# A convolution and an attention on one core: the last chunk's heads in other tiles, another loop behind the loop, and new constants for the planner of the order

## The chip, the cores and the metric

The kernel runs on one core of a Trainium2 chip. A core has TensorE (PE; its weight loads are shown as PEld), VectorE (DVE), ScalarE (ACT), GpSimd (POOL) and SyncE (SP, which here only issues DMAs), each with its own instruction stream, held together by semaphores. The metric is the device time of one execution in microseconds. Before the change it was 1152.21 us, the median of three runs (1152.09 to 1154.93).

## The reference

Two parts that share no data, and whose outputs are laid side by side:

```python
# A: S4 convolution, L = 2048, D = 576 channels, N = 128 states
P = exp(dt * (A_re + i A_im) * l);  K = einsum("dn,dnl,dn->dl", C, P, dt * B).real
y = irfft(rfft(u, 2L) * rfft(K, 2L))[:L] + u * Dskip
# B: attention, S = 2048, 32 query heads of 18, one key head and one value head
q = (x @ wq) in 32 heads;  k = x @ wk;  v = x @ wv
p = softmax(q k^T * 18 ** -0.5);  o = p v
b = concat(o over the heads) @ wo
out = concat([y, b], axis=-1)
```

## The kernel before

**Attention.** The 2048 query rows are cut into four chunks of 512 (`NCH`, `CT`). Within a chunk the 32 heads go in 8 groups of four, and within a group the keys in 16 blocks of 128. One step is one key block of one group: four heads, as two score tiles of 128 x 1024 (`scores`, L533: two matmuls each), two exponentials on ScalarE (`exponentials`, L544), and one product with the values (`product`, L846: four matmuls in four column groups, which add up over the 16 key blocks into one PSUM bank). There are 4 x 8 x 16 = 512 steps and 1024 exponentials. The values have a column of ones, so that each head's softmax denominator is row 18 of its 32 rows. After 16 steps `gather` (L547) copies the group's bank to SBUF and stores it in DRAM (`od`).

**Heads to output.** When a chunk's last group is gathered, `normalize` (L555) loads its denominators (`dn`), takes their reciprocals, stores them (`rden`), loads the heads in five blocks of rows (28 heads in four blocks m = 0 to 3 of 126 rows, the last four heads in block 4), loads each block's reciprocals broadcast over the rows (`db`) and multiplies. `outproj` (L591) then projects with `wo`: 4 row tiles x 2 column halves x 5 blocks, 40 units of one `matmul4` each. The heads lie in a single tile `oT` that all chunks share.

The last chunk is normalised block by block: block m = 0, 1, 2, 3 after groups 1, 3, 5, 6 (`LATE`, L62). Blocks 0 to 2 may be projected in the loop (`outproj_part`, L617) into an SBUF sum `part`; which (tile, half, block) units are still missing stands in `rest`. `finish` (L642) comes behind the loop: it takes the last group from PSUM (`rc_last`, `o_last`), normalises its four heads on chip with a matmul (`bc`), does all units left in `rest` and the last block with its own weights `w4`, adds them to `part` and stores the rows.

**Convolution.** It goes in 12 chunks of 48 channels. `front` (L1287) makes a chunk's kernel from powers and tables, nearly all on VectorE, with a matmul stage `kgen`; `back` (L1360) transforms input and kernel on TensorE, multiplies the spectra on VectorE, transforms back (`iy`) and stores (`outa`). The front of the next chunk and the back of this one run as two streams.

**Order.** TensorE's, ScalarE's and VectorE's orders are written out by a planner in Python when the program is built. It keeps an estimate of each engine's time (`Clock`: `K.t` for TensorE, `K.v` for VectorE, `K.a` for ScalarE) and runs the work beside the scores, exponentials and products as generators (`Stream`): `side` (query projections and output projections), `prepare` (L731: normalising), `tail` (bounds of the scores) and the convolution's streams. A generator yields what it needs next: `"v"` (VectorE, not before an estimated time), `"p"` (TensorE and the one PSUM bank for this work), `"w"` (nothing yet). `fill` (L808) puts such work between scores and products as far as a credit goes. The credit grows with each step by an allowance worked out from `TOTAL`, `LAST` and what was filled so far, between `C1` and `C2` (up to step 384) or `C3`. `RATE` is the pace of VectorE's convolution work per step, `C11` how far it may run ahead; `PACE` is the pace under which the convolution `lags` (L1491), and while it does and has a matmul waiting, no projection is begun unless it is urgent. `late` (L759) says when projections are behind, with `LEFT`. `prepare` starts a chunk's first block only when no output projection is open, and for the last chunk only when also all queries are made (`due`). Behind the loop, normalising is done to its end, then an output projection is finished, then the convolution is drained stream by stream.

Of the kernel before, what the change touches and what calls it, by code (L numbers as in the profile page):

```python
# [9 lines left out]
F32 = mybir.dt.float32  # L10
# [3 lines left out]
ALU = mybir.AluOpType  # L14
# [3 lines left out]
P = 128  # L18
# [25 lines left out]
NP = 10  # L44


RATE = 1.829
PACE = 1.71
AHEAD = 0.752
TOTAL = 429.151  # L50
LAST = 560.514

GAP = 0.437
C1, C2, C3, C4, C5, C6, C7, C8, C9, C10, C11, C12 = 0.529, 1.112, 0.728, 0.947, 0.591, 0.827, 0.566, 0.187, 0.25, 0.502, 47.793, 16.067
DEFER = 0.48
NAUG = 5
SLACK = 3.096
HEAD = 8.716

LEFT = 0.638  # L60

LATE = {1: [0], 3: [1], 5: [2], 6: [3]}  # L62

# [133 lines left out]
class Attention:  # L197
# [357 lines left out]
    def normalize(self, c, ms):  # L555

        nc, V, K = self.nc, self.V, self.k
        od = self.od[c].rearrange("(h r) n -> h r n", r=32)
        if ms[0] == 0:
            self.oT = self.cp.tile([P, 5, CT], F32, tag="oT", name=f"oT{c}")  # L560
        o = self.oT
        h0, h1 = MT[ms[0]][0] // DH, sum(MT[ms[-1]]) // DH
        n = (h1 - h0) * CT // P
        dn = self.p1.tile([P, P], F32, tag="dn", name=f"dn{c}_{h0}")
        rd = self.dr.tile([H, CT], F32, tag="rden", name=f"rden{c}_{h0}")
        nc.sync.dma_start(dn[:n, :], od[h0:h1, DH, :].rearrange("h (a n) -> h a n", n=P))
        yield "v", K.t + 8.0, False
        V.tensor_scalar(dn[:n, :], dn[:n, :], 1e-37, None, op0=ALU.max)
        V.reciprocal(dn[:n, :], dn[:n, :])
        nc.sync.dma_start(rd[h0:h1, :].rearrange("h (a n) -> (h a) n", n=P), dn[:n, :])  # L570
        for m in ms:
            m0, mn = MT[m]
            nc.sync.dma_start(o[:mn, m, :], od[m0 // DH:(m0 + mn) // DH, 0:DH, :])
        yield "v", max(K.v, K.t) + 5.0, False
        tiles = {}

        def fetch(m):
            m0, mn = MT[m]
            tiles[m] = self.p1.tile([P, CT], F32, tag="db", name=f"db{c}_{m}", bufs=2)
            nc.sync.dma_start(tiles[m][:mn, :], rd[m0 // DH:(m0 + mn) // DH, :].unsqueeze(1).broadcast_to([mn // DH, DH, CT]))  # L580
        for m in ms[:2]:
            fetch(m)
        for m in ms:
            mn = MT[m][1]
            yield "v", K.t + 7.0, False
            V.tensor_tensor(o[:mn, m, :], o[:mn, m, :], tiles[m][:mn, :], op=ALU.mult)
            self.scaled[m] = K.v + 0.3
            if m + 2 in ms:
                fetch(m + 2)

    def outproj(self, c):  # L591
        nc, V, K = self.nc, self.V, self.k
        o = self.oT
        self.o_left += 40
        yield "p", max(self.scaled[4], K.fill), False
        for t in range(4):
            ob = self.p1.tile([P, D], F32, tag="ob", name=f"ob{c}_{t}")
            for n in range(2):
                cs = slice(n * 288, (n + 1) * 288)
                ps = self.bank(288, f"op{c}_{t}_{n}")  # L600
                for m, (m0, mn) in enumerate(MT):
                    matmul4(nc, ps, o[:mn, m, t * P:(t + 1) * P], self.wo[:mn, m, cs], start=(m == 0), stop=(m == 4))
                    K.pe(0.485)
                    self.o_left -= 1
# [12 lines left out]
    def outproj_part(self, c, ms, part):  # L617

        nc, V, K = self.nc, self.V, self.k
        o = self.oT  # L620
        self.o_left += 8 * len(ms)
        for t in range(4):
            for n in range(2):
                yield "p", max(self.scaled[ms[-1]], K.fill), False
                cs = slice(n * 288, (n + 1) * 288)
                ps = self.bank(288, f"op{c}_{t}_{n}_{ms[0]}")
                for m in ms:
                    matmul4(nc, ps, o[:126, m, t * P:(t + 1) * P], self.wo[:126, m, cs], start=(m == ms[0]), stop=(m == ms[-1]))
# [12 lines left out]

    def finish(self, c, part, o_ps, w4, b4):  # L642


        nc, V, o = self.nc, self.nc.vector, self.oT
# [7 lines left out]
        def begin(t, nh, tile):  # L653

            ps[t, nh] = tile[:, :288]
            for m in range(4):
                if (t, nh, m) in self.rest:
                    matmul4(nc, ps[t, nh], o[:126, m, t * P:(t + 1) * P], self.wo[:126, m, cols[nh]], start=(m == min(x[2] for x in self.rest if x[:2] == (t, nh))), stop=False)
# [72 lines left out]
    def prepare(self):  # L731

        nc = self.nc
        while True:
# [48 lines left out]
    def main(self, conv, flag):  # L783
# [134 lines left out]
        nc.vector.tensor_scalar(flag, self.ubound[0:1, :], LIMIT / (2 * SCALE) * QQ, None, op0=ALU.is_le)  # L918
        self.finish(NCH - 1, self.part, o_ps, self.w4, self.b4)

# [678 lines left out]
```

## Time and profile before

| | |
|---|---|
| median of the runs | 1152.21 us |
| the profiled execution | 1153.4 us |
| its span (first to last instruction) | 1151.6 us |
| TensorE busy | 1085.5 us (94%) |
| ScalarE busy | 997.1 us (87%) |
| VectorE busy | 988.2 us (86%) |
| last product ends at | 1121.5 us |
| granted TensorE clock, mean | 0.99 |

Times in the views are microseconds from the span's start. A row of the timeline gives start, busy time, engine, line, operation, what is written <- what is read, shapes, how many instructions, and in brackets how long the engine was idle before it and what ended that. Each fp32 matmul stands as two records, so that a unit of an output projection, four matmuls, is eight records. `op` and `fin` are output projections in the loop and in the finish, `ops` the products, `s` the scores, `P` the exponentials. `L120`, `L124`, `L128` and `L140` are the helpers that record VectorE's operations for the planner, `L194` is `matmul4`.

### The profile page before, as it was taken

The numbers are of one execution on the slowest core, as the hardware profiler recorded it, in microseconds if no ns is written. First come the engines' busy times: TensorE is split into PE (matmuls) and PEld (weight loads), VectorE is DVE, ScalarE is ACT, GpSimd is POOL, SyncE is SP. The second block draws the span as 40 slices with busy tenths as digits, with TensorE's granted clock in tenths as the row PEclk, the third lists the DMA queues.
The fourth block names the chain that finished last, engine by engine and source line by source line (L and its number), as shares of the span: only waits on it lengthen the run. The fifth ranks groups of instructions, "written<-read, shape, count | busy, mean of one in ns | idle before, by whom it ended". The sixth has DMA issues, their size and how long they took to land.

```text
span 1151.6 us, 33003 instructions
## 1 busy us (share of the span) xinstructions
PE 1085.5 (94%) x13886; PEld 398.2 (35%) x13886; DVE 988.2 (86%) x1676; ACT 997.1 (87%) x1052; POOL 140.1 (12%) x257
## 2 busy tenths in 40 slices
PE   6989899999999999899999999999988999999996
PEld 2333234334333334333333333334222333333333
DVE  4878998997998998998899898998878898997753
ACT  3878998888989989998878899999999998999980
POOL 5321412133033010000224000000000000000000
PEclk9999999999999999999999999999989999999998
DMA  7412433122224113122212201102221202102111
GB/s 225 140 54 75 136 96 94 33 90 81 62 65 151 33 42 91 42 69 89 80 40 80 92 29 57 61 29 87 64 78 55 72 29 78 47 29 94 30 44 53
DMA packets 59279, 83.37 MB, mean 72 GB/s; under 512 B 14867, under 2 KB 35335, under 8 KB 58613
## 3 DMA queue, kind: packets, MB, share of 16 engines
q1 hardware_dynamic: 47557, 73.24, 19.8%
q0 software_dynamic: 10848, 7.37, 2.5%
q8 instruction: 111, 1.82, 0.7%
q10 hardware_dynamic: 720, 0.58, 0.2%
q14 instruction: 43, 0.35, 0.1%
HBM read 46.59 MB, written 33.85 MB: 70 GB/s over the span
## 4 chain that ended last, share of the span: by engine, by line
PE 63%; ACT 16%; DVE 11%; issue 6%; DMA 2%; POOL 1%; ACTq 0%; DVEq 0%
PE ops L846 25%; PE s L533 17%; ACT P L544 14%; PE op L194 5%; PE q L410 3%; PE kg L1280 3%; PE iy L194 3%; DVE tab L120 2%; PE fin L194 1%; POOL qd L461 1%; PE hk L194 1%; DVE ks L120 1%; DVE acc L120 1%; PE lu L194 1%; PE lk L194 1%
## 5 line engine op out<-in xcount | busy, mean ns | idle before, releaser
L544 ACT ACTIVATE P<-s 128x1024 f32<-128x1024 f32 x992 | 933.0, 1035 | 99.3 <-PE s L533 96.9
L846 PE MATMUL ops<-P,v_sb 128*32 128x512 f32 x4096 | 511.8, 599 | 2.5 <-DVE o L124 2.4
L533 PE MATMUL s<-aug,kaug 55*128 55x512 f16 x2048 | 310.2, 382 | 38.3 <-ACT P L544 32.8
L533 PEld LDWEIGHTS <-kaug 55*128 55x128 f16 x2048 | 93.6, 94 | 360.7 <-issue 317.1
L846 PEld LDWEIGHTS ops<-P,v_sb 128*32 128x32 f32 x4096 | 116.2, 110 | 162.4 <-issue 135.0
L461 POOL DMA_DIRECT2D qd<-qh x116 | 66.1, 577 | 273.8 <-DVE qh L128 271.3
L410 PE MATMUL q<-x,wq_sb 128*32 128x256 f32 x1360 | 83.7, 382 | 1.1 <-DVE ksb L124 0.6
L194 PE MATMUL op<-wo_sb,oT 126*32 126x288 f32 (+1 forms) x1024 | 73.2, 411 | 2.4 <-DVE ob L124 1.8
L1191 POOL MEMSET fr<- 128x192 f32 x24 | 9.8, 491 | 520.3 <-DVE tt L120 303.3
L120 DVE TENSOR_TENSOR tab<-tab,tt 128x576 f32<-128x576 f32 (+1 forms) x72 | 59.1, 821 | 1.7
L120 DVE TENSOR_TENSOR tab<-fr,dif 128x576 f32<-128x576 f32 (+1 forms) x72 | 58.8, 817 | 0.0
L120 DVE TENSOR_TENSOR tab<-sum,fr 128x576 f32<-128x576 f32 (+1 forms) x72 | 58.7, 816 | 0.0
L120 DVE TENSOR_TENSOR tab<-tab 128x576 f32<-128x576 f32 (+1 forms) x72 | 58.7, 815 | 0.0
L120 DVE TENSOR_TENSOR tt<-fr,sum 128x576 f32<-128x576 f32 (+1 forms) x72 | 58.6, 814 | 0.0
L410 PEld LDWEIGHTS q<-x,wq_sb 128*32 128x32 f32 x1360 | 39.5, 109 | 38.7 <-issue 14.2
L124 DVE COPY ksb<-kg 128x192 f32<-128x192 f32 x48 | 17.5, 364 | 40.4 <-PE kg L1280 39.0
L120 DVE TENSOR_TENSOR acc<-acc,pt 128x1728 f32<-128x1728 f32 (+2 forms) x36 | 48.6, 1351 | 0.3
L120 DVE TENSOR_TENSOR pt<-us,ks 128x1728 f32<-128x1728 f32 (+2 forms) x36 | 48.3, 1350 | 0.0
L1280 PEld LDWEIGHTS kg<-tab 128*32 128x32 f32 x2304 | 37.2, 111 | 25.6 <-DVE ksb L124 8.9
L542 ACT ACTIVATE P<-s,bias 128x1024 f32<-128x1024 f32 x32 | 32.9, 1121 | 13.3 <-PE s L533 13.3
L1280 PE MATMUL kg<-tab 128*32 128x64 f32 x2304 | 42.4, 222 | 0.6 <-DVE tab L120 0.3
L120 DVE TENSOR_TENSOR ks<-ks 128x576 f32<-128x576 f32 (+1 forms) x48 | 41.0, 855 | 0.9
(159 smaller groups left out, 1010.9 us busy)
## 6 DMA issues: line engine op xcount, KB each, us to landing
od<-o SPq DMA_DIRECT2D x31, 256.0 KB
aug<-qd SPq DMA_DIRECT2D x124, 55.0 KB
u<-u SPq DMA_DIRECT2D x12, 384.0 KB
kd<-ksb SPq DMA_DIRECT2D x12, 384.0 KB
kt<-kd SPq DMA_DIRECT2D x48, 96.0 KB
outa<-u SPq DMA_DIRECT2D x12, 384.0 KB
pw<-pw SPq DMA_DIRECT2D x8, 528.0 KB
oT<-od SPq DMA_DIRECT2D x16, 252.0 KB
```

The source lines that it names most:

```text
L120: return self.v.tensor_tensor(out, *a, **k)
L124: return self.v.tensor_copy(out, *a, **k)
L194: nc.tensor.matmul(ps[j:e], w[:, j:e], x, start=start, stop=stop, tile_position=(0, j))
L410: nc.tensor.matmul(ps[o, 256 * f:256 * f + 256], w[:, k, i], xt[:, k, x], start=(k == 0), stop=(k == 4), tile_position=(0, 32 * j))
L461: q.dma_start(qd[h:h + n, row + d:row + d + nd, cs], src[i1:i1 + n * nd, :cs.stop - cs.start])
L533: nc.tensor.matmul(ps[:, j, :], self.kaug[r, kb * P:(kb + 1) * P], t[r, :], start=True, stop=True)
L542: nc.scalar.activation(pt, ps, AF.Exp, bias=self.bias, scale=SCALE / QQ)
L544: nc.scalar.activation(pt, ps, AF.Exp, scale=SCALE / QQ)
L846: nc.tensor.matmul(o_ps[32 * j:32 * j + 32, :], self.v[:, kb, :], pts[2 * n + j // 2][:, j % 2, :], start=(kb == 0), stop=(kb == 15), tile ...
L1191: nc.gpsimd.memset(t[:, :, 0:NF:8], one)
L1280: nc.tensor.matmul(ps[32 * g:32 * g + 32, d, :], t[:, :32], t[:, 32:], start=(j == 0), stop=(j == 1), tile_position=(0, 32 * g))
```

## The change

- The last chunk's normalised heads go into the first 512 columns of the tiles that held the query weights of blocks 0 to 3 (`self.heads`), one tile per block; `oT` stays for chunks 0 to 2. For the last chunk `prepare` no longer waits until no output projection is open, only until all queries are made.
- `normalize` gives its steps other estimated times.
- The load of `w4` moves from block 3's preparation to the end of chunk 2's output projection.
- Behind the loop, one loop takes the step of whichever stream has its inputs first: convolution, preparing, and output while block 0 is not fully projected.
- The planner's constants are replaced.

```diff
-RATE = 1.829
-PACE = 1.71
-AHEAD = 0.752
-TOTAL = 429.151
-LAST = 560.514
-
-GAP = 0.437
-C1, C2, C3, C4, C5, C6, C7, C8, C9, C10, C11, C12 = 0.529, 1.112, 0.728, 0.947, 0.591, 0.827, 0.566, 0.187, 0.25, 0.502, 47.793, 16.067
-DEFER = 0.48
+RATE = 1.838
+PACE = 1.856
+AHEAD = 0.729
+TOTAL = 340.0
+LAST = 576.841
+
+GAP = 0.359
+C1, C2, C3, C4, C5, C6, C7, C8, C9, C10, C11, C12 = 0.549, 0.718, 0.83, 1.288, 0.739, 1.059, 0.572, 0.186, 0.382, 0.431, 24.516, 11.926
+DEFER = 0.395
 NAUG = 5
-SLACK = 3.096
-HEAD = 8.716
-
-LEFT = 0.638
+SLACK = 3.285
+HEAD = 13.454
+
+LEFT = 1.086
...
 # normalize
-        if ms[0] == 0:
-            self.oT = self.cp.tile([P, 5, CT], F32, tag="oT", name=f"oT{c}")
-        o = self.oT
+        if c < NCH - 1:
+            oT = self.oT = self.cp.tile([P, 5, CT], F32, tag="oT", name=f"oT{c}")
+            o = [oT[:, m, :] for m in range(5)]
+        else:
+            o = self.heads
...
-        yield "v", K.t + 8.0, False
+        yield "v", max(K.t + 1.0, self.o_free + 4.5) + 4.0, False
...
-            nc.sync.dma_start(o[:mn, m, :], od[m0 // DH:(m0 + mn) // DH, 0:DH, :])
-        yield "v", max(K.v, K.t) + 5.0, False
-        tiles = {}
+            nc.sync.dma_start(o[m][:mn, :], od[m0 // DH:(m0 + mn) // DH, 0:DH, :])
+        yield "v", max(K.v, K.t) + 1.6, False
+        tiles, fetched = {}, {}
 
         def fetch(m):
+            fetched[m] = max(K.t, K.v)
...
-            yield "v", K.t + 7.0, False
-            V.tensor_tensor(o[:mn, m, :], o[:mn, m, :], tiles[m][:mn, :], op=ALU.mult)
+            yield "v", max(K.t, fetched[m] + 4.6), False
+            V.tensor_tensor(o[m][:mn, :], o[m][:mn, :], tiles[m][:mn, :], op=ALU.mult)
...
 # outproj, its end
+        if c == NCH - 2:
+            self.w4 = self.p1.tile([P, D], F32, tag="ob", name="w4")
+            nc.sync.dma_start(self.w4, self.a["wo4"])
...
 # prepare
-            while ms[0] == 0 and (self.outs or c == NCH - 1 and self.due < 1 << 30):
+            while ms[0] == 0 and (self.outs if c < NCH - 1 else self.due < 1 << 30):
                 yield "w", 0.0, False
...
+                self.heads = [w.rearrange("p k n -> p (k n)")[:, :CT] for w in self.wq[:4]]
...
             if ms[0] == 3:
-                self.w4 = self.p1.tile([P, D], F32, tag="ob", name="w4")
                 self.b4 = self.p2.tile([P, P], F32, tag="aw", name="b4")
-                nc.sync.dma_start(self.w4, self.a["wo4"])
                 nc.sync.dma_start(self.b4, self.a["b4"])
...
 # main, behind the loop
-        while self.todo or self.busy or holder() or any(m == 0 for _, _, m in self.rest):
+        while True:
+            conv.turn()
+            h, live = holder(), [st for st in conv.streams if st.live]
             if self.todo or self.busy:
-                prep.advance()
-            elif holder() or self.outs:
-                (holder() or side).advance()
-        conv.drain()
+                live.append(prep)
+            if side.holds or self.outs and any(m == 0 for _, _, m in self.rest):
+                live.append(side)
+            if not live:
+                break
+            able = [st for st in live if st.kind == "v" or st.kind == "p" and h in (None, st)]
+            for st in [min(able, key=lambda st: st.event())] if able else live:
+                if st.live:
+                    K.t = max(K.t, st.event())
+                    st.advance()
```

In `outproj_part` and `finish` the heads' operand `o[:126, m, ...]` becomes `o[m][:126, ...]`.

More of the change, by code (lines that the diff above doesn't have):

```diff
@@ L615, in outproj @@
                 yield "p", K.fill, False
+        if c == NCH - 2:
+            self.w4 = self.p1.tile([P, D], F32, tag="ob", name="w4")
+            nc.sync.dma_start(self.w4, self.a["wo4"])
     def outproj_part(self, c, ms, part):
         nc, V, K = self.nc, self.V, self.k
-        o = self.oT
+        o = self.heads
         self.o_left += 8 * len(ms)
@@ L627, in outproj_part @@
                 for m in ms:
-                    matmul4(nc, ps, o[:126, m, t * P:(t + 1) * P], self.wo[:126, m, cs], start=(m == ms[0]), stop=(m == ms[-1]))
+                    matmul4(nc, ps, o[m][:126, t * P:(t + 1) * P], self.wo[:126, m, cs], start=(m == ms[0]), stop=(m == ms[-1]))
                     K.pe(0.485)
@@ L642, in finish @@
     def finish(self, c, part, o_ps, w4, b4):
-        nc, V, o = self.nc, self.nc.vector, self.oT
+        nc, V, o = self.nc, self.nc.vector, self.heads
         o_sb = self.p2.tile([P, CT], F32, tag="o", name="o_last", bufs=1)
@@ L657, in begin @@
                 if (t, nh, m) in self.rest:
-                    matmul4(nc, ps[t, nh], o[:126, m, t * P:(t + 1) * P], self.wo[:126, m, cols[nh]], start=(m == min(x[2] for x in self.rest if x[:2] == (t, nh))), stop=False)
+                    matmul4(nc, ps[t, nh], o[m][:126, t * P:(t + 1) * P], self.wo[:126, m, cols[nh]], start=(m == min(x[2] for x in self.rest if x[:2] == (t, nh))), stop=False)
         def end(t, nh):
@@ L910, in main @@
             behind += 1
-        while self.todo or self.busy or holder() or any(m == 0 for _, _, m in self.rest):
+        while True:
+            conv.turn()
+            h, live = holder(), [st for st in conv.streams if st.live]
             if self.todo or self.busy:
-                prep.advance()
-            elif holder() or self.outs:
-                (holder() or side).advance()
-        conv.drain()
+                live.append(prep)
[8 more added lines that the diff above has]
+                    st.advance()
+        self.left = len(self.rest)
+        self.left = len(self.rest)
         nc.vector.tensor_scalar(flag, self.ubound[0:1, :], LIMIT / (2 * SCALE) * QQ, None, op0=ALU.is_le)
```

## The prediction

> **What bounds the kernel now.** I read the page's busy times first, then the busy time by stretch, then who waited for whom, and last the timeline of the end and of the places where the stretches are thin. In the rows of stretches stand the stretch, its length, the busy time (and instructions) of PE, PEld, DVE, ACT and POOL, the granted clock and the DMA.
>
> ```profile
> span 1151.6 us, 33003 instructions
> PE 1085.5 (94%) x13886; PEld 398.2 (35%) x13886; DVE 988.2 (86%) x1676; ACT 997.1 (87%) x1052; POOL 140.1 (12%) x257
> ...
> 832.00:864.00 32.00, 27.06 (x237) 7.75 (x229) 24.37 (x52) 29.82 (x31) 0.80 (x2) 0.89 0.23 78
> 864.00:896.00 32.00, 27.99 (x300) 7.91 (x298) 29.05 (x43) 31.36 (x35) 0.80 (x2) 1.00 0.19 61
> 896.00:928.00 32.00, 30.20 (x424) 11.66 (x420) 26.51 (x58) 29.09 (x32) 0.00 (x0) 1.00 0.19 60
> ...
> 1056.00:1088.00 32.00, 30.73 (x386) 11.30 (x386) 20.43 (x34) 29.72 (x33) 0.00 (x0) 1.00 0.19 61
> 1088.00:1120.00 32.00, 30.44 (x318) 9.91 (x310) 21.12 (x32) 30.25 (x33) 0.00 (x0) 1.00 0.11 39
> ...
> 0.00:1121.50 1121.50, 1065.86 (x13630) 388.95 (x13634) 979.35 (x1660) 996.36 (x1050) 140.14 (x257) 0.99 0.24 73
> 1121.50:1151.60 30.10, 19.61 (x264) 9.24 (x252) 8.80 (x16) 0.77 (x2) 0.00 (x0) 0.84 0.15 51
> ```
>
> TensorE is the bound: 1085.5 of 1151.6 us, and the change leaves its matmuls the same in kind and number. So only its idle 66 us can be won, or grow: 55.6 before 1121.5, and 10.5 of the 30.1 us behind the loop, where ScalarE has almost nothing to do. In 864 to 896 the roles are swapped: ScalarE has 31.36 of 32 us and TensorE is 4.0 us short, because there is no filler (query projection, output projection, convolution) to put between the exponentials.
>
> ```profile
> PE s L533 <- ACT P L544: 32.8, 98, 2.4
> ...
> PE fin L194 <- DVE flag L918: 4.9, 1, 4.9
> ```
>
> The first row is that shortage summed over the loop, 98 small waits. The second is one wait behind it:
>
> ```profile
> 1093.12 0.68 DVE L124 COPY o<-ops 128x512 f32<-128x512 f32 x1
> ...
> 1119.62 1.90 PE L846 MATMUL ops<-P,v_sb 128*32 128x512 f32 x16
> ...
> 1120.24 0.20 DVE L128 TENSOR_SCALAR dn<-dn 28x128 f32<-28x128 f32 x1
> ...
> 1120.48 0.94 DVE L140 RECIPROCAL dn<-dn 28x128 f32<-28x128 f32 x1
> ...
> 1122.79 0.77 SPq L580 DMA_DIRECT2D db<-rden  x1
> 1126.62 0.69 DVE L120 TENSOR_TENSOR oT<-oT,db 126x512 f32<-126x512 f32 x1 [5.19 <-DMA db<-rden]
> ...
> 1127.29 0.40 DVE L675 TENSOR_SCALAR rc_last<-ops 128x256 f32<-128x256 f32 x1
> ...
> 1127.36 4.07 PE L194 MATMUL fin<-wo_sb,oT 126*32 126x288 f32 x32 [4.87 <-DVE flag L918]
> ```
>
> The last product ends at 1121.52, but the fourth block of heads (m=3) is only then normalised, through two transfers, and VectorE holds `rc_last`, the first step of the finish, behind it until 1127.29.
>
> **The change, part by part.** *Own tiles for the last heads.* Before, `prepare` (L740) lets the last chunk's first block start only when no output projection is left; the four blocks then follow one another.
>
> ```profile
> L566 SPq DMA_DIRECT2D dn<-od x4: 729/755/779, 930.3 to 1103.7; - x4
> L128 DVE TENSOR_SCALAR dn<-dn x4: 203/204/208, 1055.6 to 1120.2; 28x128 f32<-28x128 f32 x4
> ...
> L194 PE MATMUL op<-wo_sb,oT x320: 403/406/431, 927.3 to 1043.7; 126*32 126x288 f32 x128, 72*32 72x288 f32 x32
> ...
> L410 PE MATMUL q<-x,wq_sb x1360: 378/379/404, 34.7 to 614.6; 128*32 128x256 f32 x195
> ```
>
> The first denominators were asked for at 930.3 and divided at 1055.6, 125 us later, when chunk 2's projection (927.3 to 1043.7) was out of the way. Afterwards the only condition is that all queries are made; their last matmul is at 614.6, so I cost the new tiles' own waits at nothing (if the queries slip past step 416, the first block waits for them). The instructions of a block are the same: two on the denominators, one product, four transfers on SP. They are issued earlier, among the aug loads, which are made a group or more ahead. The load of `w4` moves as well, to the end of chunk 2's projection, into the tile that the last output row leaves: SP stands at it until that row is stored, with aug loads behind it. They have a group's time, over 30 us; without that the scores would wait about the 3.8 us of the `db` load below. Cost: nothing. So blocks 0 to 2 can be ready soon after groups 1, 3 and 5. For block 3, whose group's copy ends at 1093.8, the new allowances give 0.3+4.5+4.0 to the denominators, 1.2 for dividing, 1.6 and 4.6 to the product: 16.2 us, so 1110, and the loop ends at 1121.5. **Gain: the finish starts at the last product, 1127.3-1121.5 = 5.8 us.**
>
> *The clock behind the wait.*
>
> ```profile
> 816.59 2.15 PE L194 MATMUL op<-wo_sb,oT 126*32 126x288 f32 x32
> ...
> 851.35 0.39 PE L533 MATMUL s<-aug,kaug 55*128 55x512 f16 x2 [2.42 <-ACT P L544]
> ...
> 853.72 3.64 PE L846 MATMUL ops<-P,v_sb 128*32 128x512 f32 x16
> ```
>
> The 32 matmuls behind the wait took 4.07 us against 2.15 for the same 32 in the loop. **Gain: 1.9 us.** But a finish with fewer units is sparser, and a slow stretch in it is as likely: bounds 0 and +4.7 (its 64 `w4` matmuls at the 1.18 us per 16 quoted below, doubled). I take **+1.9**, the price of one such stretch, which is the nearest row. [...]
>
> *Units that leave the finish.*
>
> ```profile
> L194 PE MATMUL fin<-wo_sb,oT x192: 403/406/691, 1121.3 to 1143.6; 126*32 126x288 f32 x192
> ...
> L194 PE MATMUL op<-wo_sb,oT 126*32 126x288 f32 x320 | 23.3, 411 | 0.0
> ...
> 1127.73 1.75 DVE L678 RECIPROCAL rc_last<-rc_last 128x256 f32<-128x256 f32 x1
> ...
> 1131.36 0.96 PE L686 MATMUL bc<-rc_last,b 128*128 128x256 f32 x2
> ...
> 1132.36 0.42 DVE L672 TENSOR_TENSOR o_last<-o_last,bc 128x256 f32<-128x256 f32 x1 [2.60 <-PE bc L686]
> ...
> 1140.64 0.70 PE L692 MATMUL bc<-rc_last,b 128*128 128x256 f32 x2
> 1141.26 1.18 PE L194 MATMUL fin<-w,o_last 128*32 128x288 f32 x16
> ...
> 1143.83 2.15 PE L194 MATMUL fin<-w,o_last 128*32 128x288 f32 x32
> ```
>
> A unit is eight records, 23.3/40 = 0.58 us. The finish holds 192/8 = 24 of them, that is blocks 1, 2 and 3 whole. With the blocks ready early and chunk 2's heads sooner (below), I expect blocks 1 and 2 to be projected in the loop: 16 units leave. The finish's TensorE part now runs from 1127.29 to 1143.83+2.15 = 1145.98, 18.7 us. With 8 units left it is the chain 0.40 + 1.75 + 0.96 + 0.42, then four pairs with `w4` at 1.18 (4.7), two units between (1.2) and 0.70: 10.1 us. **Gain 8.6 us.** The output's 5.6 us behind it (1151.6-1145.98) stay. The 16 units cost 16 x 0.58 = 9.3 us in the loop, less the idle time they fill; in 1056 to 1120 that is 1.3+1.6, so I take 3 of it: **+6.3** (bounds 0, if they fall only into idle time, and 9.3).
>
> *Normalising with shorter allowances, all chunks.* A five-block chunk was given 8, 5 and 7 us a product, and is now given about 8.8, 1.6 and 4.6, two blocks to a fetch. On chunk 2 the last group is copied at 863.2, and the products run from 885.7:
>
> ```profile
> 863.22 0.69 DVE L124 COPY o<-ops 128x512 f32<-128x512 f32 x1
> ...
> L120 DVE TENSOR_TENSOR oT<-oT,db x9: 674/684/693, 885.7 to 1126.6; 126x512 f32<-126x512 f32 x8, 72x512 f32<-72x512 f32 x1
> ```
>
> Counted from the end of that copy, 863.9, the last product comes near 863.9+8.8+1.2+1.6+3 x 4.6 = 889.3, where the projection now begins at 927.3. That puts filler into the two thin stretches, which lack 4.0 and 1.8 us: **gain 2.9**, half of them (bounds 0 and 5.8). The price is VectorE arriving before a transfer. In the row at 1126.62 the product began 3.83 us after the `db` issue at 1122.79, and 1126.62-1121.42 = 5.2 us after the division; the plan allows 4.6 and 6.2. With five head loads and two fetches on SP between, it can be about 1 us late. Behind the waiting product stand VectorE's evacuations of the single filler bank, and TensorE's next filler behind these. **+1** (bounds 0 and 3, one for each of three chunks).
>
> *The loop behind the loop.* It interleaves convolution, preparing and output by what is ready. The convolution's last store is issued at 1112.46, before the last product, and m=3 is then done too, so it finds nothing to do: 0 (if the convolution slides, a rival).
>
> ```profile
> 1112.46 0.37 SPq L1440 DMA_DIRECT2D outa<-u  x1
> ```
>
> *The constants.* The planner compares the convolution's work with a multiple of the step. The trace's measure for that work is VectorE's L120 (first row) and L124 (second); the third row is tile `P`, with the exponentials under ACT:
>
> ```profile
> 0.00:586.80 586.80, 421.08 (x623) 0.99 0.28 86
> ...
> 0.00:586.80 586.80, 54.17 (x151) 0.99 0.28 86
> ...
> 0.00:586.80 586.80, 251.90 (x2016) 58.02 (x2016) 484.29 (x513) 0.99 0.28 86
> ```
>
> 513 exponentials are step 256. The work is 421+54 less 16 head copies of 0.69, or 464. RATE x 256 is 468 before and 471 after: no difference. C11 lets it be 47.8, then 24.5 us ahead; it is never ahead by as much, so that is nothing too. PACE x 256 is 438 before and 475 after: **the gate `lags` (L1491), which was open there, is closed after it**, and then the projections may start only when urgent or when no convolution matmul waits. The other constants set how much filler a step may take: TOTAL/LAST falls from 0.766 to 0.589 us per step, with a ceiling of 0.718 for 1.112 up to step 384. That spreads the same work more evenly, or starves it. I take 0 in the forecast and leave the two directions to the rivals.
>
> **Sum.** -5.8 -1.9 +1.9 -8.6 +6.3 -2.9 +1 = -10.0. The profiled execution took 1153.4 us, 1.8 over its span and 1.2 over the runs' median of 1152.2. 1153.4-10.0 = 1143.4, and on the median's scale 1142.2: I say **1142**.
>
> **Rivals.** *A: the fill becomes even.* The smaller allowance saves filler for the places that lack it. Beyond the forecast it would win what is missing in 832 to 864 (4.9) and the slow products there (3.64-1.92 = 1.7), the other half of 864 to 928 (2.9), and about as much as one of those thin stretches, 4, from the 98 small waits: 1142-13.5 = 1128.5. For it: those places are short of filler, not of time. Against: the ScalarE table loads near 845 fall where the convolution puts them, and its pace hardly changes.
>
> *B: nothing at the end.* The smaller allowance leaves block 3 or the end of the convolution behind the loop. The convolution has 9 us of room (1112.5 to 1121.5); pushed 17 us later, it takes back 8, and the 16 units stay in the finish. Only 2 or 3 us of the rest remain: about 1151.
>
> *C: slower, through `lags`.* With the gate shut, projections wait while filler runs out, and the stretch goes as 864 to 896 does, 4.0 us of TensorE idle in 32. Against the forecast's gain of 10 that decides from 80 us on (38 steps of about 2.1 us). If it held for 160 us, a seventh of the loop, it would cost 20: 1162. For it: by the work above the gate is shut most of the time. Against: the convolution is tried before the projections already when nothing is urgent, and urgent or late work passes.
>
> **How the numbers follow.** Forecast 0.45, A 0.20, B 0.15, C 0.20. For this kernel I treat 0.3%, 3.5 us, as what can be told from no change. Faster: 0.42 + 0.20 + 0.04 = 0.66. Same: 0.03 from the forecast and 0.09 of B, 0.12. Slower: C and 0.02 of B, 0.22. The forecast's own range from its bounds (clock -1.9/+2.8, units -6.3/+3.0, thin stretches -2.9/+2.9, waits -1/+2) is 1130 to 1153 if all ends fell together. To leave out no more than a fifth, the range reaches into A and C: 1126 to 1159.
>
> **What would show it.** Right: `dn` of the last chunk's first block divided near 940, not 1055; no wait for `db` behind the loop and `rc_last` within 0.5 us of the last product; `fin` with the heads down from 192 to about 64 records; the stretch behind the loop down from 30.1 to about 16 us and the loop's own end some 4 us later or unchanged. Wrong: `fin` still at 192; an `outa` store behind the last product; more than 32.8 us of score matmuls waiting for exponentials (C), or far less (A); new waits of VectorE for `db` or `dn` of more than 1 us each.

## The result and the profile after

The changed kernel takes 1143.27 us (median of four runs, 1141.65 to 1144.05) against 1152.58 us (four runs, 1152.09 to 1154.93): a ratio of 0.9913, with a 95% interval of 0.9896 to 0.9931. The forecast was 1142. The profiled execution took 1143.03 us, its span is 1141.3, which is 10.3 us less than before.

The changed kernel's page, its busy time by stretch (stretch, length, then PE, PEld, DVE, ACT, POOL, granted clock, DMA), and who waited for whom:

```profile
span 1141.3 us, 33001 instructions
PE 1083.8 (95%) x13886; PEld 397.7 (35%) x13886; DVE 988.0 (87%) x1681; ACT 998.2 (87%) x1052; POOL 139.9 (12%) x257
```

```profile
800.00:832.00 32.00, 28.85 (x390) 11.20 (x390) 23.94 (x39) 30.72 (x33) 0.00 (x0) 1.00 0.11 34
832.00:864.00 32.00, 29.65 (x238) 7.58 (x231) 31.00 (x52) 31.97 (x36) 0.82 (x2) 1.00 0.28 99
864.00:896.00 32.00, 29.45 (x360) 9.82 (x357) 28.89 (x47) 30.83 (x34) 0.00 (x0) 1.00 0.28 91
896.00:928.00 32.00, 31.26 (x442) 12.33 (x442) 25.64 (x53) 29.51 (x32) 0.81 (x2) 1.00 0.17 50
...
0.00:1120.80 1120.80, 1068.94 (x13670) 390.33 (x13674) 979.88 (x1667) 997.41 (x1050) 139.93 (x257) 0.99 0.24 73
1120.80:1141.30 20.50, 14.82 (x224) 7.37 (x212) 8.14 (x14) 0.77 (x2) 0.00 (x0) 0.95 0.18 62
```

```profile
PE s L533 <- ACT P L544: 24.6, 87, 0.5
...
DVE wq_sb L120 <- DMA db<-rden: 1.4, 1, 1.4
...
DVE oT L120 <- DMA db<-rden: 0.6, 1, 0.6
```

TensorE's work is what it was; its idle time is less. Nearly all the gain stands behind the loop: 20.5 us for 30.1. The loop's own end moved by 0.7 us, from 1121.5 to 1120.8. That is a sum of two. Tile `P` in ScalarE's stretches, the kernel before first, gives the time to the 64th exponential (32 steps) and from there to the last:

```profile
0.00:102.70 102.70, 63.13 (x65) 0.97 0.45 133
102.70:1120.40 1017.70, 902.68 (x960) 1.00 0.21 67
```

```profile
0.00:105.70 105.70, 63.36 (x65) 0.95 0.47 141
105.70:1118.90 1013.20, 903.51 (x960) 1.00 0.21 66
```

From step 33 on the changed order is 4.5 us faster; the first 32 steps were 3.0 us slower in this execution (the last section shows that these vary when the order is the same), and the last product ends 0.9 us later behind the last exponential than before. The long score waits are gone (the longest is 0.5 us, it was 2.4), and VectorE has two new waits for `db`, 2.0 us together.

The changed kernel's timeline of the end, where the last block and the finish are to be followed:

```profile
1090.44 0.68 DVE L124 COPY o<-ops 128x512 f32<-128x512 f32 x1
...
1100.96 0.20 DVE L128 TENSOR_SCALAR dn<-dn 28x128 f32<-28x128 f32 x1
...
1103.58 0.76 SPq L583 DMA_DIRECT2D db<-rden  x1
...
1110.88 0.69 DVE L120 TENSOR_TENSOR wq_sb<-wq_sb,db 126x512 f32<-126x512 f32 x1
...
1117.11 0.35 SPq L1455 DMA_DIRECT2D outa<-u  x1
...
1118.94 1.90 PE L851 MATMUL ops<-P,v_sb 128*32 128x512 f32 x16
...
1120.66 3.09 PE L194 MATMUL fin<-wo_sb,wq_sb 126*32 126x288 f32 x48
1120.91 0.42 DVE L681 TENSOR_SCALAR rc_last<-ops 128x256 f32<-128x256 f32 x1 [1.21 <-PE ops L851]
...
1133.47 2.15 PE L194 MATMUL fin<-w,o_last 128*32 128x288 f32 x32
```

Block 3 is multiplied at 1110.9, ten us before the last product ends (1120.84), and `rc_last` starts 0.07 us behind that. The convolution's last store is issued at 1117.1, still in the loop. The tiles `dn`, `op` and `fin` show how the rest of the last chunk went:

```profile
L128 DVE TENSOR_SCALAR dn<-dn x4: 204/204/206, 936.5 to 1101.0; 28x128 f32<-28x128 f32 x4
...
L194 PE MATMUL op<-wo_sb,oT x320: 402/406/431, 897.0 to 1035.4; 126*32 126x288 f32 x128, 72*32 72x288 f32 x32
L194 PE MATMUL op<-wo_sb,wq_sb x104: 403/406/431, 1044.8 to 1118.7; 126*32 126x288 f32 x104
...
L194 PE MATMUL fin<-wo_sb,wq_sb x152: 403/406/430, 1120.7 to 1133.3; 126*32 126x288 f32 x152
```

The first block's denominators are divided at 936.5 (before: 1055.6). Chunk 2's projection starts 30 us earlier, at 897.0, but ends only 8 us earlier, at 1035.4, so that the last chunk's units start at 1044.8, and only 104/8 = 13 of them are done in the loop. 19 stay in the finish.

### The profile page after: what moved, and what is told of

The parts are those of the page before. It is cut to its first block, busy times and chain, and to the rows that moved or that the text cites. A ratio compares the mean times of both kernels' runs of the same rounds, so it can differ in the third digit from the quotient of the medians.

```text
span 1141.3 us, 33001 instructions
## 1 busy us (share of the span) xinstructions
PE 1083.8 (95%) x13886; PEld 397.7 (35%) x13886; DVE 988.0 (87%) x1681; ACT 998.2 (87%) x1052; POOL 139.9 (12%) x257
## 4 chain that ended last, share of the span: by engine, by line
PE 62%; DVE 15%; ACT 12%; issue 6%; DMA 2%; POOL 1%; SPq 0%; DVEq 0%; ACTq 0%
PE ops L851 25%; PE s L533 17%; ACT P L544 12%; PE op L194 5%; DVE tab L120 4%; PE q L410 4%; PE kg L1295 3%; PE iy L194 2%; DVE ks L120 2%; DVE acc L120 2%; POOL qd L461 1%; PE hu L194 1%; PE hk L194 1%; PE fin L194 1%; PE lu L194 1%
## 5 line engine op out<-in xcount | busy, mean ns | idle before, releaser
L194 PE MATMUL op<-wo_sb,oT 126*32 126x288 f32 (+1 forms) x960 | 67.5, 410 | 3.2 <-DVE ob L124 2.5
L410 PEld LDWEIGHTS q<-x,wq_sb 128*32 128x32 f32 x1360 | 40.6, 110 | 39.1 <-issue 14.7
```

Of the source, the lines that this page charges most:

```text
L194: nc.tensor.matmul(ps[j:e], w[:, j:e], x, start=start, stop=stop, tile_position=(0, j))
L410: nc.tensor.matmul(ps[o, 256 * f:256 * f + 256], w[:, k, i], xt[:, k, x], start=(k == 0), stop=(k == 4), tile_position=(0, 32 * j))
```

## The experiments

Each ratio is against the kernel before, on the same chip, with its 95% interval. The columns behind it are read from the one profiled execution, so that they hold to about 0.1 us for that execution alone. "Loop" is the end of the last product, "steps 33 on" the time from the end of the 64th exponential to the end of the last, which is free of the start's changes, and "behind" the span behind the last product. Before: 1121.5, 1017.7 and 30.1, with 24 units in the finish; changed: 1120.8, 1013.2 and 20.5, with 19.

| run | median us | ratio | loop | steps 33 on | behind | units in the finish |
|---|---|---|---|---|---|---|
| e9_own_tiles | 1146.59 | 0.9932 (0.9915 to 0.9949) | 1120.2 | 1015.5 | 22.7 | 24 |
| e10_last_waits | 1145.79 | 0.9926 (0.9907 to 0.9945) | 1122.0 | 1017.8 | 22.8 | 24 |
| e3_shared_tile | 1142.62 | 0.9905 (0.9888 to 0.9922) | 1118.5 | 1013.4 | 21.8 | 22 |
| e1_structure | 1151.55 | 0.9981 (0.9964 to 0.9998) | 1128.1 | 1022.6 | 22.8 | 24 |
| e2_constants | 1156.03 | 1.0026 (1.0011 to 1.0041) | 1127.9 | 1022.2 | 25.3 | 18 |
| e4_old_waits | 1151.69 | 0.9992 (0.9978 to 1.0007) | 1133.2 | 1026.1 | 20.4 | 19 |
| e5_pace | 1158.57 | 1.0042 (1.0028 to 1.0057) | 1131.9 | 1029.3 | 25.7 | 21 |
| e6_budget | 1157.28 | 1.0023 (1.0006 to 1.0041) | 1136.9 | 1033.7 | 20.7 | 19 |
| e14_pace1846 | 1149.10 | 0.9963 (0.9941 to 0.9986) | 1124.3 | 1019.0 | 23.4 | 22 |
| e15_rate1840 | 1146.27 | 0.9924 (0.9897 to 0.9952) | 1124.6 | 1016.7 | 20.8 | 20 |
| e16_before_rate | 1170.19 | 1.0126 (1.0102 to 1.0149) | 1142.4 | 1040.3 | 30.9 | 24 |
| e8_finish8 | 1135.39 | 0.9857 (0.9833 to 0.9882) | 1116.0 | 1013.5 | 15.3 | 8 |

The last column says more than any single run: the finish holds 24 units in every run with the old constants (in e16 all but `RATE`), also where the last heads are ready early (e9, e1), and 18 to 22 with the new ones, also where the heads are ready late (e2, e3) and where one constant or the budget is put back; e8's 8 are left by its edit. So the constants move units out of the finish, and the own tiles and the shorter times by themselves move none. The rows of e9_own_tiles and of e2_constants (eight records a unit):

```profile
L194 PE MATMUL fin<-wo_sb,wq_sb x192: 402/406/430, 1120.0 to 1135.0; 126*32 126x288 f32 x192
L194 PE MATMUL fin<-wo_sb,oT x144: 402/406/689, 1127.7 to 1145.3; 126*32 126x288 f32 x144
```

**The structure with the old constants.**

```diff
 # the changed kernel
-RATE = 1.838
...
-LEFT = 1.086
+RATE = 1.829
...
+LEFT = 0.638
```

> The changed kernel with all planner constants of before; own tiles, new allowances in normalize, new loop behind the loop stay. Theory S (the end of the kernel pays, through block 3 being normalised in the loop): 1143 us, within 4 us of the changed kernel, and the stretch from the last product to the end again near 20.5 us (30.1 before). Rival K (the new constants pay, by spreading the filler): 1150 to 1153 us.

Measured: 1151.55 us. The stretch behind the loop is short (22.8), as theory S has it, but the loop is 9 us longer than the changed kernel's from step 33 on (5 us longer than the kernel before's) and eats most of it. Neither theory expected that. VectorE arrives before a transfer in it, by 4.3 us in one place, but TensorE's idle time next to that place is only 1.8 us, so it is a small part at most:

```profile
DVE wq_sb L120 <- DMA db<-rden: 4.3, 1, 4.3
```

**The constants alone.**

```diff
 # the kernel before
-RATE = 1.829
...
-LEFT = 0.638
+RATE = 1.838
...
+LEFT = 1.086
```

> The kernel before with all planner constants of the change and nothing else. Theory S: 1150 to 1155 us, with the wait for db behind the loop (5.19 us) still there. Rival K: 1143 to 1146 us, with the 98 small waits of the score matmuls (32.8 us) down to about 27.

Measured: 1156.03 us, slower than before beyond the interval. The wait behind the loop stays, as S expected, and again the loop is longer, 1022.2 us from step 33 on. So the constants don't pay by themselves, and rival K falls.

**Own tiles alone.**

```diff
 # the kernel before
-            while ms[0] == 0 and (self.outs or c == NCH - 1 and self.due < 1 << 30):
+            while ms[0] == 0 and (self.outs if c < NCH - 1 else self.due < 1 << 30):
...
+                self.heads = [w.rearrange("p k n -> p (k n)")[:, :CT] for w in self.wq[:4]]
...
 # normalize, outproj_part, finish: the last chunk's o[m] is self.heads[m]
 # outproj of chunk 2 loads w4
```

> The kernel before with only the own tiles, the loosened condition in prepare and the earlier w4 load; old allowances in normalize, old constants, old loop behind the loop. Theory S: block 3 is asked for at 1093 and needs 8+5+7 us of the plan, which ends near 1114, still inside the loop: 1143 to 1146 us. Rival K: 1150 to 1153 us. A third, W (the shorter allowances are needed too): block 3 is again multiplied behind the last product, 1150 us.

Measured: 1146.59 us, S's number. The loop is 2 us shorter from step 33 on, and the stretch behind it 7.4 us, with the same 24 units in the finish.

**The changed kernel with the shared tile.**

```diff
 # the changed kernel
-        if c < NCH - 1:
-            oT = self.oT = self.cp.tile([P, 5, CT], F32, tag="oT", name=f"oT{c}")
-            o = [oT[:, m, :] for m in range(5)]
-        else:
-            o = self.heads
+        if ms[0] == 0:
+            self.oT = self.cp.tile([P, 5, CT], F32, tag="oT", name=f"oT{c}")
+        o = self.heads = [self.oT[:, m, :] for m in range(5)]
...
-            while ms[0] == 0 and (self.outs if c < NCH - 1 else self.due < 1 << 30):
+            while ms[0] == 0 and (self.outs or c == NCH - 1 and self.due < 1 << 30):
```

> The changed kernel with the last chunk's heads back in the shared tile and the old condition in prepare; everything else as changed. Theory S: block 0 waits for chunk 2's projection again, but the shorter allowances (about 16 us a block for 20) may just bring block 3 to the end of the loop: 1146 to 1153 us. Rival K: 1143 to 1145 us, no different from the changed kernel.

Measured: 1142.62 us, not to be told from the changed kernel. I had given S the wrong number: block 0 waits for chunk 2's projection as before, but with the shorter times the four blocks still pass in time, and block 3 is multiplied at 1107.8, before the finish begins:

```profile
1107.84 0.69 DVE L120 TENSOR_TENSOR oT<-oT,db 126x512 f32<-126x512 f32 x1
...
1118.54 0.42 DVE L679 TENSOR_SCALAR rc_last<-ops 128x256 f32<-128x256 f32 x1 [1.21 <-PE ops L848]
```

So the new tiles are one of two ways to the same end, and with the shorter times they are not needed.

**The shorter times for the last chunk alone.**

```diff
 # the kernel before
-        yield "v", K.t + 8.0, False
+        yield "v", K.t + 8.0 if c < NCH - 1 else max(K.t + 1.0, self.o_free + 4.5) + 4.0, False
...
-        yield "v", max(K.v, K.t) + 5.0, False
+        yield "v", max(K.v, K.t) + (5.0 if c < NCH - 1 else 1.6), False
...
-            yield "v", K.t + 7.0, False
+            yield "v", K.t + 7.0 if c < NCH - 1 else max(K.t, fetched[m] + 4.6), False
```

> The kernel before with the shorter times in normalize for the last chunk alone; shared tile, old condition and old constants stay. Theory S: the four blocks, one after the other from 1055, take about 15 us each instead of 22, so block 3 is multiplied near 1108, before the last product; the stretch behind the loop falls from 30.1 to about 22.5 us and the loop stays near 1121: 1144 to 1147 us. Rival M (any mixture of old and new lengthens the loop, as in three runs): 1150 us or more.

Measured: 1145.79 us. This is the end by itself: the loop is the old one (1017.8 us from step 33 on, for 1017.7), and only what stands behind it changes. From its timeline and its stretches:

```profile
1111.98 0.69 DVE L120 TENSOR_TENSOR oT<-oT,db 126x512 f32<-126x512 f32 x1
...
1121.81 3.10 PE L194 MATMUL fin<-wo_sb,oT 126*32 126x288 f32 x48
1122.06 0.42 DVE L676 TENSOR_SCALAR rc_last<-ops 128x256 f32<-128x256 f32 x1 [1.21 <-PE ops L847]
...
1137.04 2.15 PE L194 MATMUL fin<-w,o_last 128*32 128x288 f32 x32
```

```profile
1122.00:1144.80 22.80, 17.20 (x260) 8.71 (x252) 8.15 (x14) 0.77 (x2) 0.00 (x0) 0.94 0.16 56
```

Three lines of planner times give most of the gain, 0.9926 against 0.9913, and by the intervals the two can't be told apart. e1_structure has these times and the own tiles, and is slower than e10_last_waits and than e9_own_tiles, beyond their intervals: the parts do not add up. What it has besides is the shorter times for chunks 0 to 2; no run has these alone. The same 24 units now take from 1122.06 to 1137.04+2.15 = 1139.19, 17.1 us for 18.7: the 1.6 us go with the slow matmuls behind the old wait (48 records take 3.10 here, where 32 took 4.07).

**Old times, whole loop.**

```diff
 # the changed kernel, all chunks
-        yield "v", max(K.t + 1.0, self.o_free + 4.5) + 4.0, False
+        yield "v", K.t + 8.0, False
...
-        yield "v", max(K.v, K.t) + 1.6, False
+        yield "v", max(K.v, K.t) + 5.0, False
...
-            yield "v", max(K.t, fetched[m] + 4.6), False
+            yield "v", K.t + 7.0, False
```

> The changed kernel with normalize's old times in the plan (8, 5 and 7 us). Theory F (constants and allowances were fitted as one set; a part put back lengthens the loop as it did in the two runs that mix old and new): loop end several us later than 1120.8, 1146 to 1152 us. Theory I (the parts are independent, and the allowances are worth a few us by earlier filler and VectorE waits of their own): 1141 to 1146 us. In both, block 3 is multiplied before the last product (group copied near 1090, plus 20).

Measured: 1151.69 us. The end is kept (20.4), the loop is 12 us longer in the profiled execution, which is one of the slower ones of this run; by the ratios the run is 9 us slower. Theory F holds.

**PACE back, and the budget back.**

```diff
 # the changed kernel, first run
-PACE = 1.856
+PACE = 1.71
 # the changed kernel, second run
-TOTAL = 340.0
-LAST = 576.841
-C1, C2, C3 = 0.549, 0.718, 0.83
+TOTAL = 429.151
+LAST = 560.514
+C1, C2, C3 = 0.529, 1.112, 0.728
```

> The changed kernel with PACE back at 1.71, so that the gate `lags` stays open. Rival C of the prediction (the shut gate costs): faster than the changed kernel, 1136 to 1141 us. The gate is worth nothing, as the forecast took it: 1142 to 1145 us. Theory F: slower, 1146 to 1150 us.

> The changed kernel with the filler budget of before (TOTAL, LAST, C1, C2, C3). If the smaller budget is what spreads the filler (rival A's mechanism): the thin stretch at steps 384 to 416 goes from 3.4 us of TensorE idle back to 5 or more, and 1146 to 1152 us. If the budget hardly binds: 1142 to 1145 us.

Measured: 1158.57 and 1157.28 us, both slower than the kernel before. Rival C of the prediction has the wrong sign: in this order it is the open gate that goes with the longer loop. The stretch I had named for the budget, steps 384 to 416, did not get worse: TensorE idles 3.7 us there, 3.4 in the changed kernel. The loss is spread over the loop. In e5_pace 5 us of the loss stand behind the loop: the last product ends at 1131.9, the convolution's last chunk goes on behind it, and VectorE comes to `rc_last` only at 1136.8. That is the slide of the convolution that rival B named.

Where some of the rest comes from is seen at the last burst of the convolution's powers, when ScalarE loads another table (1.28 us), computes sines and loads the exponential's table again (1.28 us), 5.6 us without an exponential. From the timelines of the changed kernel and then of e5_pace:

```profile
825.39 1.28 ACT L1163 ACT_TABLE_LOAD   x1
825.75 2.63 PE L194 MATMUL op<-wo_sb,oT 126*32 126x288 f32 x40
...
829.74 1.28 ACT L544 ACT_TABLE_LOAD   x1
...
830.12 1.66 PE L194 MATMUL op<-wo_sb,oT 126*32 126x288 f32 x24 [1.73 <-DVE ob L124]
```

```profile
868.10 1.28 ACT L1163 ACT_TABLE_LOAD   x1
...
869.14 1.92 PE L851 MATMUL ops<-P,v_sb 128*32 128x512 f32 x16
...
872.44 1.28 ACT L544 ACT_TABLE_LOAD   x1
...
874.81 0.39 PE L533 MATMUL s<-aug,kaug 55*128 55x512 f16 x2 [3.75 <-ACT P L544]
```

In the changed kernel the burst falls while eight units of output projection are still open, and TensorE does them meanwhile. In e5_pace it comes 43 us later, when chunk 1's projection is used up (it ended at 840), and TensorE waits 3.75 us. Products also wait 11.2 us for VectorE to copy the heads out, for 3.6 in the changed kernel. The planner lets a burst go as soon as eight units stand beside it, and otherwise after 16 steps. The burst comes at 822 to 825 in the changed kernel, e3_shared_tile and e15_rate1840, at 844 to 849 before and in e1, e9 and e10 (a wait of 2.4 us in each), and at 852 to 868 in e2, e4, e5, e6, e14 and e16, with waits of 2.8 to 3.8 us. It does not decide by itself: e14_pace1846 has one of the longest of these waits (3.7) and a loop of 1019.0.

**Small steps of one constant.**

```diff
 # the changed kernel, first run
-PACE = 1.856
+PACE = 1.846
 # the changed kernel, second run
-RATE = 1.838
+RATE = 1.840
 # the kernel before, third run
-RATE = 1.829
+RATE = 1.838
```

> The changed kernel with PACE 1.846 for 1.856: the gate is still shut for most of the loop (464 to 473 us of work stand against 473 at step 256). Theory G (what cost 15 us with PACE 1.71 is the open gate): 1142 to 1146 us. Theory N (any other order of the same work costs or wins some us, by where the short waits fall, and the constants pick one good order): anywhere from 1144 to 1156 us, with the loop end moved by more than 3 us and the stretch behind the loop near 20 us.

> The changed kernel with RATE 1.840 for 1.838, a change of a thousandth that still gives another order on TensorE. Theory G: 1142 to 1145 us. Theory N: 1144 to 1156 us, by the loop end alone.

> The kernel before with RATE 1.838 for 1.829 and nothing else. Theory G (such a step means nothing by itself): 1151 to 1155 us. Theory N: the loop end moves by more than 3 us from 1121.5, later more likely than earlier if before's constants were a chosen order too: 1147 to 1162 us.

Measured: 1149.10, 1146.27 and 1170.19 us. G falls with the first and the third: the first's interval lies apart from the changed kernel's, and the third is beyond even N's range. For the second the runs spread too far (1140.49 to 1150.45) to tell 3 us from nothing. Not all of the first is the loop, as N had it: its convolution ends behind the last product, and the stretch there is 23.4. A RATE half a percent higher makes the kernel before some 15 us slower by the ratio, the largest effect of all. In e16's waits, timeline and stretches (40 us each) one sees what such an order has more of:

```profile
PE ops L846 <- DVE o L124: 10.2, 8, 2.5
```

```profile
619.32 1.51 PE L1280 MATMUL kg<-tab 128*32 128x64 f32 x48 [2.59 <-DVE tab L120]
620.60 3.64 PE L846 MATMUL ops<-P,v_sb 128*32 128x512 f32 x16
```

```profile
600.00:640.00 40.00, 35.77 (x448) 12.51 (x448) 34.55 (x56) 32.01 (x35) 10.54 (x19) 0.91 0.23 74
725.00:765.00 40.00, 37.14 (x432) 12.98 (x428) 32.97 (x65) 32.77 (x36) 0.00 (x0) 0.91 0.14 45
860.00:900.00 40.00, 32.19 (x334) 9.12 (x335) 32.46 (x61) 35.72 (x37) 0.80 (x2) 0.91 0.25 82
1000.00:1040.00 40.00, 36.82 (x384) 12.23 (x376) 35.43 (x66) 32.63 (x36) 0.00 (x0) 0.91 0.12 37
```

Products wait 10.2 us for VectorE to copy the heads out (2.4 before), single ones of these waits reach 2.5 us, and in the four stretches the granted clock is 0.91: in the first of them 16 products behind the wait of 2.59 us at 619 take 3.64 us where 16 take 1.90 (at 1118.94 in the changed kernel). In the kernel before, the wait of 2.42 us at 851 is the only one over 1.5 us between 160 and 1115 us, and the granted clock is 0.50 while the 16 products behind it take their 3.64 us (853.72 to 857.36); in the changed kernel it is the 1.73 us at 830, and the clock stays at 1.00 from 820 to 840. Counting TensorE waits of 1.5 us or more between 160 and 1115 us, the faster orders have none or one (changed, e3, e9, e10, e14, e15, and the kernel before), e2 and e4 two, e5 and e6 three, e1 four, e16 seven.

**A short finish.** Only block 3's units are done in the finish; the units of blocks 1 and 2 that the changed kernel does there are left out, and with them their part of the last chunk's output.

```diff
 # the changed kernel, finish
+        self.rest = {x for x in self.rest if x[2] == 3}
```

> The changed kernel with the finish doing only block 3's units, at most 8, so 11 of the 19 are left out (their part of the output rows is missing). Theory T (TensorE's work sets the finish): 11 x 0.58 = 6.4 us less, until the chain of the prediction (10.1 us) takes over, so the finish's TensorE part falls from 14.7 to about 10.4 us and the time to about 1139 us. Rival L (the chain of reciprocal, broadcast and scaling is longer than I summed): 12 us or more, 1141 us.

```profile
1116.00:1131.30 15.30, 9.68 (x136) 4.34 (x124) 8.00 (x14) 0.77 (x2) 0.00 (x0) 0.97 0.23 82
```

Measured: 15.3 us behind the loop for 20.5, so 11 units are worth 5.2 us, 0.47 each, and TensorE's part falls to 9.6 us (theory T). By the ratios the run is 6.5 us under the changed kernel, which with the intervals of both does not differ from the 5.2. In the profiled executions the loop's end differs too, 1116.0 for 1120.8, though its order is the same instruction for instruction; from step 33 on the two agree (1013.5 and 1013.2).

**Not run.** With the old loop behind the loop put back into the changed kernel, the order of every engine stays the same, instruction for instruction; so that part of the change does nothing here. How many units the finish is left with can be read from the planner's order too. `fill` asks for more room before an output projection once more than `C7` x step + `HEAD` units are done: 297.9 at the last step before, 305.7 after. With those two constants put back in the changed kernel the planner leaves 24 units, and with those two alone set anew in the kernel before 18; with the allowance's constants put back it stays at 19, and with them alone set anew in the kernel before at 24. What such orders take on the chip was not measured.

## Why the prediction was right, and where it was not

*The finish starts at the last product, -5.8.* Measured -5.7: `rc_last` 0.07 us behind the last product, 5.77 before. e10_last_waits and e9_own_tiles each show it alone, with the loop where it was or 2 us shorter. But I gave the gain to the own tiles and their condition, and e3_shared_tile shows that they are only one way to it. What counts is that block 3 is multiplied before the last product, and that the convolution is done by then; the shorter times do the first too.

*The clock, -1.9 and +1.9.* The gain was there, 1.6 us by e10_last_waits, but the sum has it twice: the 18.7 us from which the next step takes its 8.6 hold the slow matmuls already (the granted clock is 0.50 from 1127.36 to 1131.43, over their 4.07 us), and the 10.1 hold none of these 32. The price was not there: the stretch behind the loop has a granted clock of 0.95 (0.84 before), 1.00 while TensorE works in it (1120.84 to 1135.62), and its 48 records take 3.09 us. The sparse finish that I feared does not exist: TensorE has no gap over 0.3 us in it, and none in e8_finish8's with 8 units either. So what a gap in the finish would have cost is not shown; that a slow stretch in it was as likely was my estimate. In the loop slow products stand behind waits as short as 2.42 us (before) and 2.59 us (e16), 3.64 us for 16 in both.

*16 units leave the finish, -8.6 and +6.3.* This step failed. Five left, and `fin` with the heads fell from 192 to 152 records, not to about 64; the stretch behind the loop is 20.5 us, not 16. With 24 units, no wait and 3.10 us for its first 48 records, e10's finish takes 17.1 us on TensorE, with 19 the changed kernel's takes 1133.47+2.15-1120.91 = 14.7: -2.4 in place of -8.6. The units were ready: block 0 from 946 on, block 1 from 1011. What I missed is that ready units are not done units. Chunk 2's projection started 30 us earlier and ran 138 us for 116, so it was not the supply that set its pace, and the blocks' readiness moved nothing: e9_own_tiles has blocks 0 and 1 ready at 952 and 1016 and keeps 24 units, e2_constants has block 0 ready only at 1074 and keeps 18. The filler allowance isn't it either: e6_budget puts it back and keeps 19, and e5_pace with the gate open 21. By the planner's orders it is the limit `C7` x step + `HEAD`, two of the constants that I had put at nothing as a whole. My price for a short finish was right: eight units take 9.6 us by e8_finish8 for the 10.1 summed, though as TensorE's own work, without a gap, and not as a chain of waits. A unit is worth 0.47 to 0.49 us there and takes 0.58 in the loop where it does not fall into idle time, so that moving all 16 could have won little; net I had put it at -2.3.

*The thin stretches, -2.9.* The two stretches of this term, 864 to 928, lacked 4.0 and 1.8 us of TensorE and lack 2.5 and 0.7 now: -2.5, about the size that I gave. The projection begins at 897.0, so that only the second can have it from there; in the first what is new is the transform back of a convolution chunk (`iy`, 3.0 us of TensorE), which lay at 840 to 845 before. Beside the term stands the burst, which moved from 845 to 825, where projections cover it: 832 to 864, rival A's place, lacked 4.9 us and lacks 2.4, while 800 to 832, where the burst is now, lacked 2.5 and lacks 3.2. From 800 to 928 that is -4.4 in all, as much as the loop gained from step 33 on (4.5). The first of these stretches, in the kernel before:

```profile
800.00:832.00 32.00, 29.54 (x320) 9.92 (x322) 28.57 (x37) 30.42 (x33) 0.00 (x0) 1.00 0.17 52
```


*Waits of VectorE, +1.* Two, of 1.4 and 0.6 us, the first over the 1 us that I had named as a sign of being wrong. Right in kind; e1_structure shows one of 4.3.

*The loop behind the loop, 0.* Right.

*The constants, 0.* This step failed too, and it is the one to learn from. As a whole the set costs 3 us on the old structure (e2_constants, 1.0026) and wins 8 on the new one (0.9913 against 0.9981 in e1_structure). "RATE: no difference" was argued from its meaning, half a percent of pace; in the kernel before that step of `RATE` alone costs some 15 us, and in the changed one a thousandth gives a different order. With PACE I took the shut gate for the danger (C, slower); reopening it makes the changed kernel 15 us slower. Putting back the times, the pace, the budget or all constants costs 8 to 15 us. The two whole sets have loops within 4.5 us of each other from step 33 on, and each set has one of 1022 us or more with the other's structure (e1, e2); what I called zero is the difference of two such orders, and none of the terms put back by itself (pace, budget) is near zero.

So behind the loop the sum is -5.7 (start), -1.6 (clock), -2.4 (units), together -9.7 of the 10.3 us on the spans; the loop gives 0.7, which is -4.5 from step 33 on and +3.8 ahead of that and in its last products. The forecast had -14.4 behind the loop (-5.8 -1.9 +1.9 -8.6) and +4.4 in it (+6.3 -2.9 +1); measured are -9.6 and -0.7. Two misses of about 5 us cancel. The direction and the wait behind the loop are right by their mechanism; that the number came out within 2 us is luck, and the constants' 0 was not earned by its argument.

What stays open is why a given constant gives a given loop. The bursts without cover and the waits for head copies show where the time goes in e5 and e16; that they make up all of the difference is not shown, since no run moved the burst and nothing else. No run that does all the work beats the changed kernel beyond its interval.

## What to carry to other kernels

Look first at what stands on an otherwise idle engine behind the last loop: a late chain of two transfers cost 7 us here, and three lines of earlier planned times took it away without touching the loop. Where an order is worked out by a greedy planner, a constant can't be priced by its meaning: change one, and the whole order changes, so measure the set with the structure, and try a small step of one constant to see how far an order falls by chance. And before counting on work that moves into a full loop, ask what sets its pace there: work that is ready earlier is not done earlier where a limit of the planner holds it back.

## What the runs showed of the hardware

The same order took different times in the loop: 1120.8 us in the profiled execution of the changed kernel, 1116.0 in that of e8_finish8. The same two stretches as above, for e8_finish8:

```profile
0.00:100.60 100.60, 63.35 (x65) 1.00 0.50 148
100.60:1114.10 1013.50, 903.42 (x960) 1.00 0.21 66
```

The first 32 steps took 100.6 us here and 105.7 there, at a granted clock of 1.00 and 0.95; the 480 steps behind them took 1013.5 and 1013.2. So the whole difference of these two executions comes from the start, where TensorE is busy 86.1 of the first 100 us in the changed kernel's execution (921.4 of the 956 from 160 to 1116). The granted clock was 0.50 there in three stretches (29.9 to 33.2, 60.6 to 64.0 and 91.4 to 94.7), and 1.00 over the same 32 steps of e8_finish8; these two profiled executions are 5 us apart before the part that was changed begins. The table's column from step 33 on is made for that; how much the later steps vary between executions of the other orders is not shown, as each has one trace.
